# Another order of the passage between two stages, gathers asked for one block per step, and a last step in pieces

## The chip, the cores and the metric

The kernel runs on one core of a Trainium2 chip, in one launch. The metric is the device time of one execution in microseconds (us). The engines are TensorE (PE; its weight loads have a row of their own, PEld), VectorE (DVE), ScalarE (ACT), GpSimd (POOL) and SyncE (SP); each takes its instructions in program order and waits for others by semaphores. SP issues the ordinary DMAs, POOL issues the gathers and scatters by index.

## The reference

Three layers follow each other. The first is a recurrent attention over 4 x 8 heads of 768 steps and 40 dimensions, with an input gate, a forget gate and an output gate per step:

```python
m_new = np.maximum(f_gate[:, :, t] + m, i_gate[:, :, t])
C = f_stab * C + i_stab * einsum('bhd,bhe->bhde', vt, kt)
n = f_stab * n + i_stab * kt
y[:, :, t] = o * (C @ q) / max(abs(n @ q), 1)
```

Its output, 3072 rows of 320, goes through a mixture of 8 experts (hidden width 1024): a row is normed and compared with eight expert vectors, and only the best expert computes, `gate_w * (relu(x @ w1[e]) @ w2[e])`. The third layer is gated: `(sigmoid(x @ w_gate) * (x @ w_val)) @ w_out` with a hidden width of 1536. Everything is float32, the last layer's weights come as float64.

## The kernel before, in words

Products are made of float16 or bfloat16 pairs: each operand is split into a high part and what is left (low), and three products are added up. The splits are work for ScalarE (the high part, a copy) and for VectorE or GpSimd (the low part, a subtraction). The order of all instructions is written out by hand, so the order of calls in the program is the order on every engine.

**Attention.** The steps are cut into 6 chunks of 128, with 4 batches each: 24 tiles, numbered by `i`. For a tile `st_V` (GpSimd) weights V, `st_V2` splits it (copy `vh` on ScalarE, subtraction `vl` on GpSimd, for tile 22 on VectorE), `st_S` makes the scores and splits them (`ah`, `al`), `st_AV` multiplies, `st_post` divides and gates on VectorE (L574 to L567), `st_XT` turns the rows (`tp_x`), copies them (`xt`, ScalarE), squares them with a sum (L600, ScalarE) and stores them to `xs` in memory. `st_logit` makes the eight logits, `st_route` marks the best expert per row, `st_rank` counts rows per expert over a chunk and returns a list of operations (`rk`) that write the "marks" `oh_p` and `oh_b`: where in its expert's list a row stands. The last of the list is a ScalarE copy of `oh_b` (L668). `st_index` multiplies the marks into the row list (`ix_ps`), `st_first` makes the gather indices of the first expert from it.

**The passage** (from L1543 on) is the stretch in which the last four tiles (20 to 23, `t0 + 0` to `t0 + 3`) end and the first expert begins. `split_w1(0, p)` and `split_w2(0, p)` return the copies (`c10`, `c20`, ...) and the subtractions (`l10`, ...) for part `p` of the first expert's weights; a part of `w1` serves two of its eight hidden blocks. `load_w1` and `load_w2` ask for the next part over SP, once the raw buffer is read. `fill(u, n)` puts `n` matmuls on constants (L1533), whose result nobody reads. `half()` advances the first expert by half a step: its product for one hidden block (L1030 to L1034), or the activation `hh` (ScalarE, L1127), its low part `hl` (VectorE, L1128) and the second-layer products of two blocks before (L1043 to L1048).

**The experts.** They run in order of their size, with windows of 512 to 336 rows as columns; the first one in two runs of 256, the first of them over rows of all chunks but the last two. `expert_steps(n)` does run `n` in eight steps, one per hidden block `f`. In a step stand, in this order: the products, the gathers of the next run's rows (`load_x`, at `f == 0` all three or four blocks of 128 rows, L756 on GpSimd), the copies and subtractions of weight parts that come next (`w1l` L247, `w2l` L261, float64 pieces of the last layer L1212, tails `w1s` and `w2h` L216 on VectorE), and from step 3 on the scaling of the next run's gathered rows, one block a step (L990, ScalarE). From run 2 on each step takes one operation of `defer`, a list that makes the output's places: stores to `permd`, a load back, a copy to float (`pf`, L1339) and a transpose (`pn_ps`, L1314).

**The gated layer** takes 72 steps (six groups of 512 rows, twelve blocks of 128 hidden units). In a step `gated_a` and `gated_b` make gate and value products in two halves of the array at once (64 rows each), then sigmoid (L1833), product with the value (L1834), cast `hh` (L1846) and low part `hl` (L1847) follow, and `gated_l2h` multiplies by `w_out` two steps later. In the last step these four are done in two pieces of 256 columns (`col_parts`), then the output products of the last two steps follow block by block (`gated_l2`), each block is scaled (ScalarE or VectorE in turn, L1908 and L1906) and scattered to its rows by GpSimd (L1926).

Of the kernel before, what the change touches and what calls it, by code (L numbers as in the profile page):

```python
# [22 lines left out]
def kernel(  # L23
# [431 lines left out]
    def st_V2(i):  # L455
        t = vV[i]
        vh = bp.tile([P, H, DV], F16, tag="vh", name="vh")
        vl = bp.tile([P, H, DV], F16, tag="vl", name="vl")
        nc.scalar.copy(vh, t)
        (nc.vector if i == NTILE - 2 else nc.gpsimd).tensor_tensor(out=vl, in0=t, in1=vh, op=ALU.subtract)  # L460
        vV[i] = (vh, vl, t)

# [125 lines left out]

    def st_XT(i):
# [10 lines left out]
        nc.scalar.activation(out=jk, in_=xr[:, 0:DM], func=AF.Square, accum_out=ssq[:, i:i + 1])  # L600
# [683 lines left out]
    def place_ops():  # L1284
# [27 lines left out]
        def turn_back():  # L1312
# [25 lines left out]
            none,  # L1338
            lambda: v.tensor_copy(pf, pl),  # L1339
            turn_back,  # L1340
# [98 lines left out]
    def expert_steps(n):  # L1439
# [50 lines left out]
        for f in range(NF1):  # L1490
# [3 lines left out]
            if f == 0 and more:  # L1494
                load_x(n + 1)
# [53 lines left out]
    st_S(t0 + 3)  # L1549
    st_AV(t0 + 1)  # L1550
    st_logit(t0 - 1)
    st_V(t0 + 3)
    st_V2(t0 + 2)
    st_sig(t0 + 2)
    weave(c10)
    st_route(NCH - 2)
    st_post(t0 + 1)
    fill(0, 4)
    st_XT(t0)
    fill(0, 6)  # L1560
    transpose_part(0, xt[0], 0)
    st_V2(t0 + 3)
    st_sig(t0 + 3)
    weave(l10)
    load_w1(0, 2)
    fill(0, 4)
    st_AV(t0 + 2)
    weave(c20, l20)
    load_w2(0, 2)
    fill(0, 2)  # L1570
    st_logit(t0)
    rk = st_rank(NCH - 2)
    rk.pop(0)()
    transpose_part(0, xt[0], 1)
    st_post(t0 + 2)
    fill(1, 2)
    transpose_part(0, xt[0], 2)
    weave(c11[0:1], l11[0:1])
    fill(1, 2)
    st_XT(t0 + 1)  # L1580
    weave(c11[1:], l11[1:])
    load_w1(0, 3)
    fill(1, 2)
    st_AV(t0 + 3)
    st_post(t0 + 3)
    st_XT(t0 + 2)
    st_logit(t0 + 1)
    half()
    st_XT(t0 + 3)
    weave(rk)  # L1590
    half()
    st_logit(t0 + 2)
    st_logit(t0 + 3)
    st_route(NCH - 1)
    half()
    weave(c21, l21)
    load_w2(0, 3)
    rk = st_rank(NCH - 1)
    weave(rk[0:5])
    half()  # L1600
    half()
    weave(rk[5:])
    weave(*split_w1(0, 2))
    load_w1(1, 0)
    half()
    half()
    half_, low = split_w1(0, 3, nc.vector)
    weave(half_)
    st_index(NTILE - 2 * B, NTILE)
    st_first(E0 // P, GT)  # L1610
    load_x(1)
    half()
# [6 lines left out]
    half()  # L1619
    work += weight_ops()  # L1620
# [199 lines left out]
    def gated_b(t):  # L1820
        g, f = order2[t]
        fs = slice(f * P, (f + 1) * P)
        for kk in range(2):
            ins = woven(*(
                products(r, ps, w, xg[g], kk, fs, stop=(kk == 1))
                for r, ps, w in zip(halves, gv[t][::-1], gate_val[::-1])
            ))
            if kk == 0:
                turn_rows(ins[0], t)
# [9 lines left out]
    def col_parts(t):  # L1839
        return [slice(0, NM)] if t < last else [slice(u * NM // 2, (u + 1) * NM // 2) for u in range(2)]  # L1840
# [539 lines left out]
```

## Time and profile before

| | |
|---|---|
| three timed runs | 716.05 us median (714.97 to 717.76) |
| profiled execution | 710.32 us, span 708.4 us |
| busy share of the span | PE 96%, PEld 61%, DVE 60%, ACT 59%, POOL 46% |
| mean granted TensorE clock | 0.996 |
| passage and first expert run | about 113 to 151 us in the span |
| experts' runs 1 to 8 | about 150 to 343 us |
| gated layer | about 343 us to the end |

A row of a timeline gives start and length in us, engine, line of the kernel, operation, the tile written and the tiles read, the shape, and in brackets how long the engine had stood idle before it and who released it. Several like instructions in a row are merged (x6).

### The profile page before, as it was taken

To read this page: it belongs to the slowest core of one execution; us is meant where nothing else is said; L and a number is where in the kernel's file an instruction comes from. 1 tells how busy PE (TensorE), PEld (TensorE's weight loads), DVE (VectorE), ACT (ScalarE), POOL (GpSimd) and SP (SyncE) were. 2 spreads that over 40 slices of the span, in tenths; PEclk is the share of its full clock that TensorE was granted. 3 is DMA by queue.
4 is the path that set the end of the run, shared out by engine and by line. 5 is a ranking of instruction groups with operands and counts; after the bars stand their busy time and mean duration, and the time that the engine had idled before them with its cause. 6 is when DMAs were issued, how large, how long until landed. Compare 5 with 4: busy or idle time off the path is not lost. (4 is left out here: it accounts for less than half of the span.)

```text
span 708.4 us, 17936 instructions
## 1 busy us (share of the span) xinstructions
PE 681.5 (96%) x6955; PEld 434.4 (61%) x6955; DVE 424.7 (60%) x924; ACT 418.9 (59%) x1059; POOL 327.4 (46%) x392
## 2 busy tenths in 40 slices
PE   6999999899999989899999999999999999999994
PEld 5899998786445545566555555555545557755552
DVE  7978888688689998887798875252221122211111
ACT  5887876766966767678566455454555453433331
POOL 8968887544754666565010003443234324324222
PEclk9999999999999999999999999999999999999998
DMA  7756975456455557661233220010000001001001
GB/s 222 225 185 176 278 227 157 128 177 190 123 149 158 174 170 201 178 187 56 57 84 86 65 75 24 17 39 1 2 19 20 1 2 38 2 2 39 1 2 41
DMA packets 39865, 70.47 MB, mean 99 GB/s; under 512 B 4818, under 2 KB 28460, under 8 KB 39772
## 3 DMA queue, kind: packets, MB, share of 16 engines
q1 hardware_dynamic: 36764, 59.61, 28.5%
q0 software_dynamic: 3008, 9.64, 4.2%
q8 instruction: 56, 0.92, 0.5%
q14 instruction: 37, 0.30, 0.1%
HBM read 60.55 MB, written 8.68 MB: 98 GB/s over the span
## 5 line engine op out<-in xcount | busy, mean ns | idle before, releaser
L1834 DVE SCALAR_TENSOR_TENSOR sgm<-v_ps,sgm 128x512 f32<-128x512 f32 (+1 forms) x73 | 49.8, 684 | 197.1 <-ACT sgm L1833 197.0
L1847 POOL TENSOR_TENSOR hl<-sgm,hh 128x512 f16<-128x512 f32 x54 | 62.3, 1159 | 210.7 <-ACT hh L1846 210.6
L1790 PE MATMUL v_ps<-xg,wvh 64*128 64x512 f16 x288 | 108.5, 377 | 1.9 <-ACT seen L1804 1.8
L1790 PE MATMUL g_ps<-xg,wgh 64*128 64x512 f16 x288 | 108.5, 377 | 0.0
L1791 PE MATMUL g_ps<-xg,wgh 64*128 64x512 f16 x288 | 108.3, 376 | 0.0
L1791 PE MATMUL v_ps<-xg,wvh 64*128 64x512 f16 x288 | 108.3, 376 | 0.0
L1792 PE MATMUL g_ps<-xg,wgl 64*128 64x512 f16 x288 | 108.3, 376 | 0.0
L1792 PE MATMUL v_ps<-xg,wvl 64*128 64x512 f16 x288 | 108.3, 376 | 0.0
L1872 PE MATMUL o_ps<-wo,hl 64*128 64x320 f16 x560 | 86.1, 296 | 0.5 <-POOL hl L1847 0.5
L1871 PE MATMUL o_ps<-wo,hh 64*128 64x320 f16 x560 | 86.2, 296 | 0.0
L1870 PE MATMUL o_ps<-wo,hh 64*128 64x320 f16 x560 | 86.2, 296 | 0.0
L1833 ACT ACTIVATE sgm<-g_ps 128x512 f32<-128x512 f32 (+1 forms) x73 | 43.0, 591 | 72.6 <-PE g_ps L1792 72.6
L1846 ACT CAST hh<-sgm 128x512 f16<-128x512 f32 (+1 forms) x73 | 44.6, 612 | 43.5 <-DVE sgm L1834 42.7
L1804 ACT COPY seen<-zeros 1x1 f32<-1x1 f32 x142 | 26.8, 189 | 64.4 <-PE o_ps L1872 34.2
L261 POOL TENSOR_TENSOR w2l<-w2raw,w2h 128x512 bf16<-128x512 f32 x28 | 35.0, 1249 | 39.0 <-issue 19.2
L1044 PE MATMUL y_ps<-hl,w2h 128*128 128x256 f16 (+7 forms) x144 | 46.8, 325 | 3.0 <-DVE hl L1128 3.0
L1127 ACT ACTIVATE hh<-h_ps 128x256 f16<-128x256 f32 (+7 forms) x72 | 35.0, 486 | 24.2 <-PE h_ps L1034 23.8
L1032 PE MATMUL h_ps<-xh,w1l 128*128 128x256 f16 (+7 forms) x144 | 46.8, 325 | 1.0 <-POOL w1l L247 1.0
L1030 PE MATMUL h_ps<-xh,w1h 128*128 128x256 f16 (+7 forms) x144 | 46.8, 325 | 0.2 <-ACT w1h L244 0.2
L1043 PE MATMUL y_ps<-hh,w2h 128*128 128x256 f16 (+7 forms) x144 | 46.8, 325 | 0.0
L1031 PE MATMUL h_ps<-xl,w1h 128*128 128x256 f16 (+7 forms) x144 | 46.8, 325 | 0.0
L1045 PE MATMUL y_ps<-hh,w2l 128*128 128x256 f16 (+7 forms) x144 | 46.8, 325 | 0.0
(381 smaller groups left out, 1976.6 us busy)
## 6 DMA issues: line engine op xcount, KB each, us to landing
kv<-in_kvo_dram SPq DMA_DIRECT2D x24, 484.0 KB
w2raw<-in_moe_w_dram SPq DMA_DIRECT2D x32, 320.0 KB
w1raw<-in_moe_w_dram SPq DMA_DIRECT2D x32, 256.0 KB
qk<-in_qkt_dram SPq DMA_DIRECT2D x48, 160.0 KB
xs<-x SPq DMA_DIRECT2D x24, 192.0 KB
w1raw<-in_moe_w_dram SPq DMA_DIRECT2D x64, 64.0 KB
raw<-in_moe_w_out_dram SPq DMA_DIRECT2D x12, 320.0 KB
raw<-in_moe_w_gate_dram SPq DMA_DIRECT2D x8, 384.0 KB
```

Source lines behind the costliest of these rows:

```text
L1030: nc.tensor.matmul(ps, hi[:, kk, fs], h[:, kk], start=(kk == 0), stop=False)
L1031: nc.tensor.matmul(ps, hi[:, kk, fs], l[:, kk], start=False, stop=False)
L1032: nc.tensor.matmul(ps, lo[:, kk, fs], h[:, kk], start=False, stop=False)
L1043: nc.tensor.matmul(ys[d], wh, hh, start=first, stop=False)
L1790: lambda: nc.tensor.matmul(ps, at(wh), h[rows, kk], start=start, stop=False),
L1791: lambda: nc.tensor.matmul(ps, at(wh), l[rows, kk], start=False, stop=False),
L1792: lambda: nc.tensor.matmul(ps, at(wl), h[rows, kk], start=False, stop=stop),
L1834: nc.vector.scalar_tensor_tensor(out=s[:, cs], in0=pv[:, cs], scalar=2.0 ** -KH, in1=s[:, cs], op0=ALU.mult, op1=ALU.mult)
L1847: e.tensor_tensor(out=gl[:, cs], in0=s[:, cs], in1=gh[:, cs], op=ALU.subtract)
L1870: lambda: nc.tensor.matmul(o, gh[rows, ts_], wh[rows], start=begin, stop=False),
L1871: lambda: nc.tensor.matmul(o, gh[rows, ts_], wl[rows], start=False, stop=False),
L1872: lambda: nc.tensor.matmul(o, gl[rows, ts_], wh[rows], start=False, stop=end),
```

## The change

- In the passage the calls stand in another order. V of the last two tiles is weighted and copied before the scores of tile 23, and the subtraction `vl` of tile 22 is put between two operations of `st_S`. The last four tiles' output and turning come earlier, the ranks of the last-but-one chunk later. The copies of weight parts 2 and 3 of `w1` stand before the last marks of the last chunk (`rk[5:]`). Of the fillers 10 are left of 22. The squares of the last four tiles are kept in a list and made later, in twos.
- `load_x` is called for one block in each of the steps 0 to 3.
- In `place_ops` the copy `pf` stands two empty entries later, and the transpose one more entry behind it.
- In the last gated step `gated_b` makes the first half of the columns for both row pieces, then the second; `col_parts` gives 128, 128 and 256 columns; the outputs of the last group are scaled by both engines, 192 columns on ScalarE and 128 on VectorE.

```diff
@@ -452,13 +452,16 @@
         )
         vV[i] = t
 
-    def st_V2(i):
+    def st_V2(i, apart=False):
         t = vV[i]
         vh = bp.tile([P, H, DV], F16, tag="vh", name="vh")
         vl = bp.tile([P, H, DV], F16, tag="vl", name="vl")
         nc.scalar.copy(vh, t)
-        (nc.vector if i == NTILE - 2 else nc.gpsimd).tensor_tensor(out=vl, in0=t, in1=vh, op=ALU.subtract)
         vV[i] = (vh, vl, t)
+        low = lambda: (nc.vector if i == NTILE - 2 else nc.gpsimd).tensor_tensor(
+            out=vl, in0=t, in1=vh, op=ALU.subtract
+        )
+        return low if apart else low()
 
     def warm(n):
 
@@ -586,6 +589,8 @@
     def st_post(i):
         weave(post_ops(i))
 
+    squares = []
+
     def st_XT(i):
         tp = tp_ps("tp_x")
         xr = xX[i]
@@ -597,7 +602,13 @@
         if i >= NTILE - B:
             nc.scalar.copy(xr[:, DM:DX], xr[:, 2 * P:DM])
         jk = bp.tile([P, DM], F32, tag="jk", name="jk", bufs=1)
-        nc.scalar.activation(out=jk, in_=xr[:, 0:DM], func=AF.Square, accum_out=ssq[:, i:i + 1])
+        square = lambda: nc.scalar.activation(
+            out=jk, in_=xr[:, 0:DM], func=AF.Square, accum_out=ssq[:, i:i + 1]
+        )
+        if i < NTILE - B:
+            square()
+        else:
+            squares.append(square)
         nc.sync.dma_start(out=xs[i * P:(i + 1) * P, :], in_=xX.pop(i))
 
     def st_logit(i):
@@ -1336,7 +1347,10 @@
                 out=pl, in_=permd[0:NT].rearrange("(i p) o -> i (p o)", p=P)
             ),
             none,
+            none,
+            none,
             lambda: v.tensor_copy(pf, pl),
+            none,
             turn_back,
             lambda: v.tensor_copy(perm, ps[1][:, 0:NTILE]),
         ]
@@ -1491,8 +1505,8 @@
             next(run_)
             if f == NF1 - 1 and more:
                 next(run_)
-            if f == 0 and more:
-                load_x(n + 1)
+            if more and f < len(blocks(n + 1)):
+                load_x(n + 1, (f,))
             prepare(f)
             if n == 1:
                 m = min(3, len(work) - 4)
@@ -1546,69 +1560,67 @@
     st_AV(t0)
     st_post(t0)
     st_sig(t0 + 1)
-    st_S(t0 + 3)
+    st_V(t0 + 3)
+    low = st_V2(t0 + 2, True)
+    st_S(t0 + 3, None, low)
     st_AV(t0 + 1)
     st_logit(t0 - 1)
-    st_V(t0 + 3)
-    st_V2(t0 + 2)
+    st_V2(t0 + 3)
+    st_post(t0 + 1)
     st_sig(t0 + 2)
     weave(c10)
-    st_route(NCH - 2)
-    st_post(t0 + 1)
-    fill(0, 4)
+    weave(l10)
+    load_w1(0, 2)
+    fill(0, 2)
     st_XT(t0)
     fill(0, 6)
+    st_AV(t0 + 2)
+    st_sig(t0 + 3)
+    st_post(t0 + 2)
     transpose_part(0, xt[0], 0)
-    st_V2(t0 + 3)
-    st_sig(t0 + 3)
-    weave(l10)
-    load_w1(0, 2)
-    fill(0, 4)
-    st_AV(t0 + 2)
+    fill(1, 2)
+    st_AV(t0 + 3)
     weave(c20, l20)
     load_w2(0, 2)
-    fill(0, 2)
+    st_route(NCH - 2)
+    st_post(t0 + 3)
+    st_XT(t0 + 1)
     st_logit(t0)
-    rk = st_rank(NCH - 2)
-    rk.pop(0)()
     transpose_part(0, xt[0], 1)
-    st_post(t0 + 2)
-    fill(1, 2)
+    weave(c11[0:1], l11[0:1])
     transpose_part(0, xt[0], 2)
-    weave(c11[0:1], l11[0:1])
-    fill(1, 2)
-    st_XT(t0 + 1)
+    st_XT(t0 + 2)
     weave(c11[1:], l11[1:])
     load_w1(0, 3)
-    fill(1, 2)
-    st_AV(t0 + 3)
-    st_post(t0 + 3)
-    st_XT(t0 + 2)
     st_logit(t0 + 1)
-    half()
+    rk = st_rank(NCH - 2)
     st_XT(t0 + 3)
-    weave(rk)
-    half()
+    weave(rk[:-1])
     st_logit(t0 + 2)
     st_logit(t0 + 3)
+    weave(rk[-1:])
     st_route(NCH - 1)
+    half()
     half()
     weave(c21, l21)
     load_w2(0, 3)
+    half()
     rk = st_rank(NCH - 1)
     weave(rk[0:5])
     half()
-    half()
-    weave(rk[5:])
-    weave(*split_w1(0, 2))
+    c12, l12 = split_w1(0, 2)
+    weave(c12, l12)
     load_w1(1, 0)
     half()
+    acts, low = split_w1(0, 3, nc.vector)
+    weave(acts)
+    weave(rk[5:])
     half()
-    half_, low = split_w1(0, 3, nc.vector)
-    weave(half_)
+    half()
     st_index(NTILE - 2 * B, NTILE)
     st_first(E0 // P, GT)
     load_x(1)
+    weave(squares[0:2])
     half()
     half()
     weave(low)
@@ -1617,6 +1629,7 @@
     load_w2(1, 0)
     half()
     half()
+    weave(squares[2:])
     work += weight_ops()
     st_slots()
     nc.scalar.activation(out=dum, in_=zeros[:, 0:1], func=AF.Exp)
@@ -1820,13 +1833,14 @@
     def gated_b(t):
         g, f = order2[t]
         fs = slice(f * P, (f + 1) * P)
-        for kk in range(2):
-            ins = woven(*(
-                products(r, ps, w, xg[g], kk, fs, stop=(kk == 1))
-                for r, ps, w in zip(halves, gv[t][::-1], gate_val[::-1])
-            ))
-            if kk == 0:
-                turn_rows(ins[0], t)
+        for cs in ([slice(0, NM)] if t < last else [slice(u * NM // 2, (u + 1) * NM // 2) for u in range(2)]):
+            for kk in range(2):
+                ins = woven(*(
+                    products(r, ps[:, cs], w, [z[:, :, cs] for z in xg[g]], kk, fs, stop=(kk == 1 and cs.stop == NM))
+                    for r, ps, w in zip(halves, gv[t][::-1], gate_val[::-1])
+                ))
+                if kk == 0 and cs.start == 0:
+                    turn_rows(ins[0], t)
         pg, pv = gv.pop(t)
         s = mw.tile([P, NM], F32, tag="sgm", bufs=2, name="sgm")
         for cs in col_parts(t):
@@ -1837,7 +1851,7 @@
         return s
 
     def col_parts(t):
-        return [slice(0, NM)] if t < last else [slice(u * NM // 2, (u + 1) * NM // 2) for u in range(2)]
+        return [slice(0, NM)] if t < last else [slice(a, b) for a, b in ((0, P), (P, 2 * P), (2 * P, NM))]
 
     def gated_h(t, s):
         gh, gl = (mw.tile([P, NM], F16, tag=z, name=z, bufs=3) for z in ("hh", "hl"))
@@ -1901,8 +1915,12 @@
 
     back = 2.0 ** -(KX + KW - KH + KD)
 
-    def scaled_out(dst, o, j):
-        if j % 2:
+    def scaled_out(dst, o, j, both=False):
+        if both:
+            c = 3 * DM // 5
+            nc.scalar.activation(out=dst[:, 0:c], in_=o[:, 0:c], func=AF.Copy, scale=back)
+            nc.vector.tensor_scalar_mul(dst[:, c:], o[:, c:], back)
+        elif j % 2:
             nc.vector.tensor_scalar_mul(dst, o, back)
         else:
             nc.scalar.activation(out=dst, in_=o, func=AF.Copy, scale=back)
@@ -1921,7 +1939,7 @@
                     out=ot[g][:, j], in0=o, scalar=back, in1=part(g, j), op0=ALU.mult, op1=ALU.add
                 )
             else:
-                scaled_out(ot[g][:, j], o, j)
+                scaled_out(ot[g][:, j], o, j, g == NG - 1)
             i = g * G4 + j
             put = nc.gpsimd.indirect_dma_start(
                 out, bass.IndirectOffsetOnAxis(perm[:, i:i + 1], 0), ot[g][:, j], None,
```

## Rows read from the trace of the kernel before

**Rows 1.** Page: busy time of TensorE; granted clock (tenths) in 40 slices.
```profile
PE 681.5 (96%) x6955; PEld 434.4 (61%) x6955; DVE 424.7 (60%) x924; ACT 418.9 (59%) x1059; POOL 327.4 (46%) x392
...
PEclk9999999999999999999999999999999999999998
```

**Rows 2.** Waits of TensorE, whole span: total us, times, longest us.
```profile
PE y_ps L1044 <- DVE hl L1128: 3.0, 2, 1.9
PE pn_ps L1314 <- DVE y L1339: 2.0, 1, 2.0
...
PE r_ps L626 <- DVE sel L619: 0.3, 1, 0.3
...
PE h_ps L1030 <- ACT w1h L244: 0.2, 1, 0.2
```

**Rows 3.** The tile that the fillers write: count, ns, first and last start.
```profile
L1533 PE MATMUL fill_ps<-ones_bf x22: 376/379/379, 119.2 to 127.5; 128*128 128x512 bf16 x22
```

**Rows 4.** Timeline of TensorE in the passage: start, us, instruction, idle before.
```profile
120.41 1.46 PE L1533 MATMUL fill_ps<-ones_bf 128*128 128x512 bf16 x6
...
137.88 0.28 PE L704 MATMUL ix_ps<-oh_b,oh_p 128*128 128x64 bf16 x4 [0.41 <-ACT oh_b L668]
...
140.68 0.28 PE L1032 MATMUL h_ps<-xh,w1l 128*128 128x256 f16 x1 [1.00 <-POOL w1l L247]
```

**Rows 5.** Timeline of ScalarE in the passage.
```profile
128.57 0.47 ACT L600 ACTIVATE jk<-x 128x320 f32<-128x320 f32 x1
...
131.77 0.48 ACT L595 COPY xt<-tp_x 128x384 f32<-128x384 f32 x1 [0.86 <-PE tp_x L593]
...
137.46 0.37 ACT L668 ACTIVATE oh_b<-r_ps,pcol 128x128 bf16<-128x128 f32 x1 [2.39 <-DVE oh_b L667]
137.73 0.41 ACT L221 ACTIVATE w1s<-w1raw 128x256 f16<-128x256 f32 x1
...
138.61 0.62 ACT L244 CAST w1h<-w1raw 128x512 f16<-128x512 f32 x1
```

**Rows 6.** Timeline of VectorE, windows of the fifth and sixth expert.
```profile
257.35 4.92 DVE L216 SCALAR_TENSOR_TENSOR w1s<-w1raw,w1s 64x256 f16<-64x256 f32 x1
...
283.16 3.20 DVE L216 SCALAR_TENSOR_TENSOR w2h<-w2raw,w2h 128x128 f16<-128x128 f32 x1
```

**Rows 7.** Timeline of GpSimd, window of the fifth expert.
```profile
253.90 1.31 POOL L756 DMA_INDIRECT xrow<-xs,idx  x1
...
257.73 0.92 POOL L1212 TENSOR_TENSOR wvl<-fa,wvh 128x384 f16<-128x384 f32 x1
...
260.83 1.14 POOL L247 TENSOR_TENSOR w1l<-w1raw,w1h 128x512 bf16<-128x512 f32 x1
```

**Rows 8.** Timeline of all engines, the last output blocks.
```profile
696.56 0.10 PEld L1893 LDWEIGHTS <-hl 128*128 128x128 f16 x1 [0.35 <-DVE hl L1847]
...
697.62 0.99 POOL L1926 DMA_INDIRECT out_dram<-ot,perm  x1 [4.52 <-ACT ot L1908]
...
701.51 0.98 POOL L1926 DMA_INDIRECT out_dram<-ot,perm  x1 [0.31 <-issue]
```

**Rows 9.** Busy us by stretch at the end; granted clock, DMA share, GB/s last.
```profile
701.00:703.00 2.00, 0.00 (x0) 0.00 (x0) 0.00 (x0) 0.00 (x0) 1.18 (x2) 0.94 0.30 98
703.00:705.00 2.00, 0.00 (x0) 0.00 (x0) 0.00 (x0) 0.00 (x0) 0.00 (x0) 0.50 0.26 91
```

**Rows 10.** VectorE's tail subtraction of w1, all: min, median, max ns.
```profile
L216 DVE SCALAR_TENSOR_TENSOR w1s<-w1raw,w1s x29: 421/422/4921, 141.4 to 325.7; 64x256 f16<-64x256 f32 x29
```

**Rows 11.** Timeline of VectorE, then TensorE, window of the second run.
```profile
154.09 1.70 DVE L172 TENSOR_TENSOR sf_r<-sq_y,rs 128x24 f32<-128x24 f32 x1
...
166.27 0.27 PE L1044 MATMUL y_ps<-hl,w2h 128*128 128x256 f16 x1 [1.15 <-DVE hl L1128]
```

**Rows 12.** Gathers between 250 and 330 us: from start to landing.
```profile
DMA to landing us min/median/max: 3.3/3.5/4.4
```

**Rows 13.** Timeline of ScalarE, window of the seventh expert.
```profile
314.63 0.61 ACT L990 ACTIVATE xrow<-xrow,gsl 128x384 f32<-128x384 f32 x1
```

## The prediction

> **What bounds the kernel now.** I read the page's busy times first: TensorE is busy for 96% of the span [rows 1], so time is won only where TensorE stands, or where what it runs is not needed. Next the waits of TensorE, who was waited for and for how long [rows 2]: the reader is to see three that lie in what the diff touches, 3.0 us before the second expert product (two waits, the longest 1.9), 2.0 us before one small transpose, and a handful of short ones in the passage. Then the passage itself, in time order for each engine. There TensorE seems never idle, but 22 of its matmuls are fillers on constants [rows 3]; six of them take 1.46 us with the last one's 0.38 in it, so they follow each other at 0.215 us. At the end of the passage it stands for the second mark (oh_b) and for part 2 of the first-layer weights [rows 4]. ScalarE, which makes both, has two holes shortly before, 0.86 and 2.39 us [rows 5]. For the two long waits I followed VectorE and GpSimd in the windows of the fifth and sixth expert [rows 6, 7], and for the end the last output blocks [rows 8].
>
> **Passage.** The diff takes 12 of 22 fillers out (16 + 6 become 8 + 2): 12 x 0.215 = 2.6 us of TensorE [rows 3, 4]. That counts only if the chain beside it gets shorter too, so I work out both sides up to the place where TensorE starts the second half of the index products, now 137.88 [rows 4].
>
> TensorE's side: 137.88 less its own wait 0.41, less 2.6, less the 0.33 before the ranks [rows 2] = 134.5. New holes come back: the last two logit products wait for ScalarE's copies of the turned rows, which now stand behind the second weight copy; by laying the rows end to end I get about 0.35 and 0.5. It arrives near 135.4.
>
> ScalarE's side: the second mark runs at 137.46 [rows 5]. Ahead of it are moved the three copies of part 2 (from 137.73, the last at 138.61 with some 0.5 to the next, so 1.4 us) and two of part 3 (0.8 us): +2.2. Behind it go four squares, 0.47 each [rows 5]: -1.9. The two holes, 3.25 us, are now where the copies stand, for the row attention's last tiles are finished earlier (their low part of V is made before the scores' last subtraction, VectorE's ranks come later): -3.25. New holes, waiting for the last logits and the first expert product, again laid end to end: +1.0. Sum -1.9 or -2.0: the mark starts near 135.5, takes 0.37, and index goes on near 135.9. The two sides meet within half a microsecond, so neither the fillers nor the copies alone give it. Index comes 2.0 us earlier; behind it the waits of 0.25 and 1.00 for the part-2 weights [rows 2, 4] go as well, since their copies stand a whole mark earlier and GpSimd's subtractions (0.67 and 1.15 us) follow at once. That is 2.0 + 1.25 = 3.25 us. The row list of experts' second half (index, first, two gathers) moves by the same 2 to 3.5, so its small wait after it stays about as it is. Bounds: 3.85 if all fillers and waits go with only the holes of 0.85 in their place; 0 if the part-3 weights land late and hold up mark and index (no row shows when they land). I take 3.2, nearer to the upper end, as it is the one that rows carry.
>
> The fillers could be what keeps the clock up. The granted clock is full, that is 2.4 GHz, in every slice of the page up to the last [rows 1], those of the waits of 1.9 and 2.0 us with them; it falls only at the end, where TensorE does nothing after its last product at 699.0: 0.94 from 701 to 703, then 0.50, the 1.2 GHz level [rows 9]. My longest new hole is near 0.5. The Trainium skill, "TensorE: Matmul & The Clock Gate" (What's actually happening), states that an array left idle falls back to half its clock; by it fewer fillers are a risk (rival d), and the trace agrees as far as its end goes.
>
> **Rows asked one block per step.** In the fifth window GpSimd issues three gathers in a row from 253.90, 1.25 to 1.6 us each, and its four subtractions for the weights queue up: from 257.73 to 261.97 they run without a gap [rows 7]. VectorE's subtraction of the weight tail, 0.42 us in the median of 29 [rows 10], has two inputs in SBUF and takes 4.92 us, to 262.27: just until that pile is through [rows 6]. Behind it stands hl, and TensorE waits for it: 1.9 us. In the sixth window it is the same with 3.20 us, and there the copy of the places (L1339) is queued behind it, for which the transpose waits 2.0 us [rows 2]. With one gather per step the order on GpSimd is gather, two subtractions, gather, one, gather, one. VectorE gets in at the first gather: its operations beside the first two gathers of this window took their normal time. That is at 259.25 in place of 262.27 by the same rows, hl about 2.5 us earlier than now and 0.7 before TensorE asks for it. In the sixth window it gets in at 283.35, and the transpose has in addition been put two steps behind its copy, steps of 2.6 us. So 1.9 + 2.0 = 3.9 go; what is late next is hl of the fourth hidden block, which by my laying out comes 0.3 before it is wanted, so I leave 0.4 standing and take 3.5. Moved past: the later gathers now stand in front of later subtractions, each up to 1.25 us later, for weights needed two or more steps on. Bounds 1.9 and 4.0.
>
> In run 1 (second half of the first expert; the gate's factors are worked out beside it) VectorE is busy without a hole for 15 us and TensorE waits 1.15 us for it once; one small VectorE operation is stretched to 1.70 us by GpSimd's subtraction [rows 11]. The four subtractions fall on other VectorE operations after the change; I find one that loses 1.5 us less and two that lose more. I take 0, from -0.6 to +1.0.
>
> The Trainium skill, "SBUF — State Buffer" (Who interferes with whom), says that of VectorE with two SBUF inputs and GpSimd the first to start holds the pair of ports for its whole instruction. Taken alone this would let VectorE in after one subtraction. By that the pile would cost VectorE no more than one subtraction, and the spreading would win little: the 3.5 would be about 0.5 and the time 711.8. The rows show it kept out through four [rows 6, 7], so I keep 3.5.
>
> **Last gated step.** The six pairs of the value and gate products become twelve of half the columns, at 0.107 instead of 0.215 us each (by columns; 256-column products elsewhere step by 0.109): the same 1.3 us, at most 0.1 more. Sigmoid and product of the first two blocks can start before the second half is through. ScalarE does its three sigmoids before its first cast, so the first cast waits for the second half all the same, but it is then 128 columns, not 256: hh and hl of block 0 are there about 0.3 us before TensorE comes, and its waits for them, 0.35 for hl [rows 8] and about as much for hh, go. The first output's scaling, split over two engines, is 0.1 us shorter. The first scatter starts at 697.1 for 697.62. The four scatters follow each other at 1.30 us (697.62 to 701.51) [rows 8], and that row of four sets the end; it moves as a whole: 0.5 us. Bounds 0 (if the sigmoid waits for the whole bank) and 0.7.
>
> **Sum.** 3.2 + 3.5 + 0 + 0.5 = 7.2 us. The profiled execution is 710.32 us (span 708.4 and 1.9 around it), so 703.1 for one profiled like this; the median of the runs is 716.05, 5.7 above the profiled one. I apply the same difference to the median: 708.8.
>
> **Rivals.**
> (a) The pile comes back. GpSimd's three subtractions of the sixth window become ready at 282.2, 283.4 and 284.8, and would nearly touch even without gathers; if VectorE does not get in at a gather, it loses up to 1.2 us at each of them. For: VectorE was held from 257.35 on, 0.4 before the gather's row ended. Against: the normal durations beside other gathers. Price: the 3.5 shrinks to 0.5; 711.8.
> (b) The copies in front of the second mark wait for the part-3 weights, which are asked for behind GpSimd's second subtraction and compete with the row stores. Then mark, index and the second half's rows come later and the passage gives 0.5 to 1: 711.3. Against: the request is made over 1 us earlier than now, as the second subtraction ends earlier.
> (c) The other sign: the rows of a next window, asked for at the step f, are scaled by ScalarE at f + 3. A gather lands 3.3 to 4.4 us after its start [rows 12]; in the narrow windows (2.4 us a step) GpSimd comes to the third gather 4 to 5 us later than now, and the row scaling at 314.63 [rows 13] would stand before it, with every hidden block behind it. It decides from 1.2 us of wait in each of six windows, 7.2 in all; with 2 us each the time is 716.05 - 7.2 + 12 = 720.9. By my rows the third gather of the seventh window starts near 309.7 and lands at 313.0 to 314.1, 0.5 to 1.6 in front; so it costs nothing, with little to spare.
> (d) The clock falls in the passage. Half clock over the 15 us of the first expert block costs 7.5: 716.3. Against are the rows above.
> (e) The change does little: (a) and (b) together, 714.3.
>
> **Chances.** Forecast 0.60, (a) 0.13, (b) 0.12, (e) 0.09, (c) 0.04, (d) 0.02. What a measurement here can tell from no change is 0.5%, 3.6 us. Faster by more: the forecast, (a) and (b), which lie at 708.8 to 711.8, nearly whole: 0.83. Within: (e) and a rest of the others: 0.12. Slower: 0.05. The range goes from 705.8 (upper bounds: 3.85 + 4.0 + 1.0 + 0.7 = 9.6, and some scatter of the runs) to 713.0 (past (a) and (b)).
>
> **What would show it.** Passage: no filler behind about 124, index ending near 136, no wait before the fifth block's first product; a wait for oh_b over 1 us, or ScalarE standing for w1raw, means (b). Windows: no VectorE tail subtraction above 2 us, hl and the transpose gone from TensorE's waits; long ones still there mean (a). ScalarE idle in front of the row scaling, ended by a gather, means (c). A granted clock below 1.00 between 120 and 140 means (d). End: first scatter about 0.5 us nearer to the last product, no waits between the last products.

## The result, and the profile after

| | median | runs | ratio of after to before (95% interval) |
|---|---|---|---|
| before | 716.30 us | 6 (714.97 to 718.82) | |
| after | 710.18 us | 6 (709.01 to 712.18) | 0.9913 (0.9889 to 0.9937) |

The change takes 6.1 us (4.5 to 8.0 by the interval); forecast were 7.2 us and 708.8. The profiled execution after took 709.01 us (span 707.0 us), 1.2 below the median of its runs. That of before was 5.7 below the median of its first three, so the two profiles differ by 1.3 us only. Experiment 1 shows why; where sizes are compared below, its second profile of before stands beside the first.

First the waits of TensorE after (total us, times, longest), which answer to [rows 2]:

```profile
PE v_ps L1803 <- ACT seen L1817: 3.8, 8, 1.9
PE y_ps L1055 <- DVE hl L1139: 1.7, 2, 1.1
...
PE o_ps L1884 <- ACT seen L1817: 1.4, 1, 1.4
PE r_ps L637 <- ACT xt L600: 0.9, 1, 0.9
PE sp_ps L1010 <- DVE xl L216: 0.6, 1, 0.6
PE tp_x L598 <- ACT rs L622: 0.5, 1, 0.5
...
PE tp_m L1028 <- DVE perm L1355: 0.2, 1, 0.2
```

The 2.0 us before the transpose of the places are gone, and the two waits for hl that are left belong to products of run 1 (256 columns), not to the fifth window. Gone too are the waits for weight part 2. New are 0.9 and 0.5 us for copies of ScalarE in the passage. The timeline of TensorE there:

```profile
128.36 0.18 PE L637 MATMUL r_ps<-sel,tri_bf 128*128 128x32 bf16 x1 [0.88 <-ACT xt L600]
...
129.21 0.55 PE L598 MATMUL tp_x<-ident,x 128*128 128x128 f32 x3 [0.50 <-ACT rs L622]
...
132.22 0.42 PE L1041 MATMUL h_ps<-xh,w1h 128*128 128x256 f16 x1
...
137.16 0.62 PE L715 MATMUL ix_ps<-oh_b,oh_p 128*128 128x64 bf16 x8
```

For the index products no wait is listed any more, where before the second four began at 137.88 behind one of 0.41 [rows 4]. But a product of 256 columns takes 0.42 us at 132.22, where its like at 131.02 takes 0.27. The same stretch in windows of 2 us (length, busy time, granted clock, DMA share, GB/s):

```profile
130.00:132.00 2.00, 2.00 (x16) 0.88 0.77 265
132.00:134.00 2.00, 2.00 (x13) 0.50 0.80 248
134.00:136.00 2.00, 2.00 (x23) 0.76 0.00 1
```

The granted clock fell to the lower of its two levels, 1.2 GHz, for some 3 us, behind the two holes (the first slower product starts at 131.45): rival (d), to which I gave 0.02.

In the fifth window VectorE's subtraction of the weight tail takes 1.11 and 1.91 us, no longer 4.92 [rows 6]. VectorE first, with the operation that is now held longest there, then GpSimd:

```profile
255.58 1.11 DVE L216 SCALAR_TENSOR_TENSOR w1s<-w1raw,w1s 64x256 f16<-64x256 f32 x1
...
258.39 1.91 DVE L216 SCALAR_TENSOR_TENSOR w1s<-w1raw,w1s 64x256 f16<-64x256 f32 x1
...
260.61 3.05 DVE L1205 TENSOR_SCALAR fb<-raw 128x384 int32<-128x384 int32 x1
```
```profile
255.50 0.92 POOL L1223 TENSOR_TENSOR wvl<-fa,wvh 128x384 f16<-128x384 f32 x1 [2.05 <-ACT wvh L1222]
256.37 1.34 POOL L247 TENSOR_TENSOR w1l<-w1raw,w1h 128x512 bf16<-128x512 f32 x1
257.86 0.96 POOL L767 DMA_INDIRECT xrow<-xs,idx  x1
258.84 1.16 POOL L261 TENSOR_TENSOR w2l<-w2raw,w2h 128x512 bf16<-128x512 f32 x1
260.17 0.97 POOL L767 DMA_INDIRECT xrow<-xs,idx  x1 [0.16 <-issue]
261.14 1.17 POOL L247 TENSOR_TENSOR w1l<-w1raw,w1h 128x512 bf16<-128x512 f32 x1
262.26 1.17 POOL L261 TENSOR_TENSOR w2l<-w2raw,w2h 128x512 bf16<-128x512 f32 x1
```

At the end TensorE's last gate product, ScalarE's and VectorE's shares of the first output block, the first of four scatters and VectorE's share of the second block, which answer to [rows 8]:

```profile
693.00 0.27 PE L1805 MATMUL g_ps<-xg,wgl 64*128 64x256 f16 x1
695.15 0.33 ACT L1921 ACTIVATE ot<-o_ps 128x192 f32<-128x192 f32 x1 [0.16 <-PE o_ps L1907]
695.51 0.29 DVE L1922 TENSOR_SCALAR ot<-o_ps 128x128 f32<-128x128 f32 x1
696.08 0.99 POOL L1944 DMA_INDIRECT out_dram<-ot,perm  x1 [4.39 <-DVE ot L1922]
696.33 0.29 DVE L1922 TENSOR_SCALAR ot<-o_ps 128x128 f32<-128x128 f32 x1 [0.52 <-ACT ot L1921]
```

From product to scatter it is 3.08 us; before, the same distance was 3.33 (694.29 to 697.62). VectorE starts 0.03 us after ScalarE's share has ended; at the second block the row names ScalarE's share as what it waited for.

For all experiments one table of stretches, read from TensorE's timelines: from the first index product of the first half (near 112) to run 1's first row turning (`tp_m`), then from turning to turning, and the gated layer from its first gate product to the start of its last output product. Where a cell holds the clock's fall, that is said.

| kernel | passage | run 1 | 5th | 6th | 7th window | gated |
|---|---|---|---|---|---|---|
| before, first profile | 35.37 | 15.21 | 26.68 | 24.31 | 20.22 | 357.47 |
| before again (exp. 1) | 35.36 | 14.83 | 26.67 | 23.20 | 20.22 | 361.63 |
| after | 33.39, falls | 15.39 | 24.68 | 22.27 | 20.64 | 361.09 |
| passage alone (2) | 33.27, falls | 15.57 | 26.67 | 23.19 | 20.22 | 362.04 |
| windows alone (3) | 35.36, falls | 15.14 | 24.68 | 22.27 | 20.68 | 362.40 |
| last step alone (4) | 35.38 | 15.12 | 26.69 | 25.85, falls | 20.23 | 361.36 |
| holes filled (5) | 32.42 | 15.43 | 24.67 | 22.27 | 20.66 | 361.83 |
| product early (6) | 32.76, falls | 14.63 | 24.69 | 22.27 | 20.67 | 361.04 |
| gathers at once (7) | 34.90, falls | 15.11 | 26.68 | 22.26 | 20.23 | 361.11 |
| places early (8) | 33.49, falls | 15.34 | 24.68 | 22.27 | 20.22 | 361.70 |
| product and fillers (9) | 32.38 | 14.63 | 24.69 | 22.26 | 20.23 | 361.10 |
| mark first (10) | 32.08 | 14.71 | 24.68 | 22.27 | 20.23 | 361.80 |
| fewer fillers (11) | 35.39, falls | 15.13 | 26.68 | 23.19 | 20.23 | 361.67 |
| whole scaling (12) | 32.36 | 15.38 | 24.68 | 22.27 | 20.22 | 361.05 |

Run 2 takes 30.5 to 30.9 us in all eight profiles with one gather per step, and 31.4 to 31.5 in five of the six with all gathers at the first step; the first profile of before, with 30.5, is the sixth. In experiment 1 the 0.9 us more stand at two waits that a profile with one gather per step doesn't have:

```profile
173.56 0.38 PE L1043 MATMUL y_ps<-hh,w2h 128*128 128x512 f16 x1 [0.21 <-ACT hh L1127]
174.28 0.38 PE L1044 MATMUL y_ps<-hl,w2h 128*128 128x512 f16 x1 [0.35 <-DVE hl L1128]
```

Run 3 (29.1 to 30.4) varies with either order, run 4 is 26.4 and the eighth run 21.6 in all.

### The profile page after: what moved, and what is told of

Its sections match the earlier page's. It is cut to its first block, busy times and chain, and to the rows that moved or that the text cites. A ratio compares the mean times of both kernels' runs of the same rounds, so it can differ in the third digit from the quotient of the medians.

```text
span 707.0 us, 17947 instructions
## 1 busy us (share of the span) xinstructions
PE 681.2 (96%) x6955; PEld 428.1 (61%) x6955; DVE 424.8 (60%) x928; ACT 419.7 (59%) x1063; POOL 328.1 (46%) x392
## 5 line engine op out<-in xcount | busy, mean ns | idle before, releaser
L1884 PE MATMUL o_ps<-wo,hh 64*128 64x320 f16 x560 | 84.9, 296 | 1.4 <-ACT seen L1817 1.4
L1885 PE MATMUL o_ps<-wo,hh 64*128 64x320 f16 x560 | 84.9, 296 | 0.0
L247 POOL TENSOR_TENSOR w1l<-w1raw,w1h 128x512 bf16<-128x512 f32 x31 | 37.6, 1211 | 20.8 <-ACT w1h L244 19.7
L479 PE MATMUL s_ps<-qk 40*128 40x128 f32 (+1 forms) x384 | 42.1, 300 | 4.5 <-DMA qk<-in_qkt_dram 4.3
```

Source lines behind the costliest of these rows:

```text
L1884: lambda: nc.tensor.matmul(o, gh[rows, ts_], wh[rows], start=begin, stop=False),
L1885: lambda: nc.tensor.matmul(o, gh[rows, ts_], wl[rows], start=False, stop=False),
```

## Experiments

**1. The kernel before, once more.** No edit.

> The kernel before, unchanged, once more, with a profile of its own. Theory: its first profile (710.32 us) is 4.6 us shorter than its fastest timed run, and these microseconds are stray delays that most executions have and that one had not. Then the ratio is 1.000 within 0.002, the new profile reads between 714 and 717 us, and it shows the difference to the first one in a few places that the change doesn't touch. Rival: the profiled execution is shorter by its nature; then it reads 710 to 711 again, with the same waits in the same places.

714.79 us against 714.98, ratio 1.0001 (0.9987 to 1.0014); span 712.2 us. Two stops in the gated layer, where ScalarE had been away, are in this profile and not in the first. TensorE, then ScalarE:

```profile
537.15 0.39 PE L1790 MATMUL v_ps<-xg,wvh 64*128 64x512 f16 x1 [1.85 <-ACT seen L1804]
...
596.21 0.31 PE L1870 MATMUL o_ps<-wo,hh 64*128 64x320 f16 x2 [1.38 <-ACT seen L1804]
```
```profile
533.67 0.60 ACT L1833 ACTIVATE sgm<-g_ps 128x512 f32<-128x512 f32 x1 [2.66 <-remote]
```

The twelve profiles of after and of the other experiments have these two stops as well; the first profile of before alone is without, by the table 4.2 us shorter in that layer. The theory holds, and the wait in the sixth window is 0.9 here where the first profile had 2.0. What stops ScalarE is not shown by the trace ("remote" is no instruction of the kernel).

**2 to 4. Each part alone.** (2) The passage's edits; (3) `load_x` one block per step and the places later; (4) the last gated step.

> The new order of the passage alone (fillers, weight copies ahead of the last marks, squares later); gathers at the first step and the last gated step as before. Theory: the passage gives 2.0 us where its end is read (the clock at half speed for some 3 us takes 1.5 of the predicted 3.2), and run 1 keeps its waits: 1.5 to 2.5 us faster than before, ratio 0.9965 to 0.998. Rival: what the passage gives is taken back by the two waits of the fifth and sixth expert window, which follow from where GpSimd's work falls; then 0 to 1 us.

> Only the gathers asked for one block per step and the places' copy and transpose later; passage and last gated step as before. Theory: the pile on GpSimd is the cause of the two long waits; both go (VectorE's tail subtractions below 2 us, no wait of TensorE above 0.5 us in the fifth and sixth window), run 1 is unchanged or 0.5 worse: 3.0 to 4.0 us faster, ratio 0.9944 to 0.9958. Rival: the windows owe part of their gain to the passage, which moves all later work; then one of the two waits stays at over 1 us and the gain is 1.5 to 2.5.

> Only the last gated step by halves and the outputs' split scaling. Theory: the end is nearer by 0.25 us, which a comparison can't tell from nothing: ratio 0.999 to 1.000; last product to first scatter 3.1 us for 3.3. Rival: the predicted 0.5 us.

| part | ratio | by times | by the table |
|---|---|---|---|
| passage (2) | 0.9988 (0.9975 to 1.0001) | -0.9 us | -2.1 in the passage, +0.4 to +0.7 in run 1 |
| windows (3) | 0.9945 (0.9928 to 0.9962) | -3.9 us | -2.0, -0.9 (first profile: -2.0), +0.5, and -0.9 in run 2 (first profile: 0) |
| last step (4) | 0.9996 (0.9982 to 1.0010) | -0.3 us | last product to scatter 3.09 |

The sum of the three by times is 5.1 us, the whole 6.1, within the intervals. Expectations (3) and (4) were met. That of (2), 1.5 to 2.5 us, was missed: -0.9 (-1.8 to +0.1) has the size of its rival, but not for the rival's reason. In (2) the waits of the fifth window (1.89) and the sixth (0.85) stand as in experiment 1: the passage's gain is not taken back there (0.4 to 0.7 of it are missing in run 1), and by (3) the windows need nothing from the passage. In (4) the clock fell from 288 to 294 (0.79, 0.50, 0.85), behind the wait of 1.84 for the places: so this wait can cost more than its length, which neither profile of before had shown.

**5. The holes of the passage filled.**

```diff
     st_logit(t0 + 1)
+    fill(1, 4)
     rk = st_rank(NCH - 2)
+    fill(1, 2)
     st_XT(t0 + 3)
```

> The changed kernel with six more fillers (4 and 2, 0.215 us each) in the two holes that TensorE has before the ranks and before the last tile's turning in the passage (0.88 and 0.50 us); they cost 1.29 us of TensorE where it stands for 1.38. Theory: those holes bring the clock to half speed for some 3 us behind them; filled, the granted clock stays 1.00 from 130 to 136, the first expert's end comes 1.0 to 1.5 us earlier than in the changed kernel: ratio to before 0.989 to 0.990 (the changed kernel: 0.991). Rival 1: the clock falls with the fillers too, since few-column products, not the holes, lead to it; then the same time as the changed kernel or 0.2 worse. Rival 2: the clock stays up, but the second mark on ScalarE sets the index's time anyway, and nothing is gained.

Ratio 0.9886 (0.9863 to 0.9910), 708.68 us; the interval overlaps that of after, so the comparison rests on the profiles. In the passage the clock stays up:

```profile
130.00:132.00 2.00, 1.94 (x21) 1.00 0.83 202
132.00:134.00 2.00, 2.00 (x20) 1.00 0.90 313
134.00:136.00 2.00, 2.00 (x27) 1.00 0.54 181
```

and the passage is 0.97 us shorter than after (32.42 for 33.39; 1.0 to 1.5 were expected), though TensorE runs 1.29 us more of products that nobody reads. It is not the full 1.5 that the slow products cost after (16 of them, from 131.45 to 134.97 less the ranks between, take 3.26 us for 1.74 at 0.109), since TensorE now waits for the mark:

```profile
138.04 0.28 PE L715 MATMUL ix_ps<-oh_b,oh_p 128*128 128x64 bf16 x4 [0.66 <-ACT oh_b L679]
```

So both the theory and a part of rival 2 hold: with the holes filled the clock stays up, and behind that stands ScalarE's chain.

**6. The first product in the first hole.** One `half()` moved from behind `st_route(NCH - 1)` to before `rk = st_rank(NCH - 2)`.

> The changed kernel with the first expert's product for its first hidden block (eight products, 0.87 us) ahead of the ranks, so that useful work stands in the hole of 0.88 us in place of fillers. Theory: TensorE gains up to 0.65 us, and with only one hole of 0.5 left the clock stays at 1.00; together 1.0 to 2.0 us less than the changed kernel, ratio to before 0.988 to 0.990. Rival: ScalarE's row of copies before the second mark becomes what the index waits for; then TensorE waits over 0.5 us for oh_b and the gain over the changed kernel is 0.3 to 0.9.

Ratio 0.9894 (0.9870 to 0.9917). The passage is 0.63 us shorter than after, but the clock falls here too (0.50 from 132 to 134), behind holes of 0.19 and 0.30 us and at one of 0.39. The expectation's 1.0 us was not reached in the passage (it is 1.39 with run 1, whose length varies), and what it was built on didn't hold: three short holes are left, not one of 0.5.

**7 and 8. The two edits of the windows apart.** (7) all gathers at the first step again; (8) the places at their old steps.

```diff
 (7)
-            if more and f < len(blocks(n + 1)):
-                load_x(n + 1, (f,))
+            if f == 0 and more:
+                load_x(n + 1)
```

> The changed kernel with all gathers of a next window asked for at its first step, as before; passage, last gated step and the later copy of the places as changed. Theory: the pile on GpSimd is the gathers' own: VectorE's tail subtractions take over 3 us again, the fifth window's wait of 1.9 us comes back, and the sixth's is smaller than before (2.0) because the transpose waits two steps longer: 2 to 4 us slower than the changed kernel, ratio to before 0.994 to 0.997. Rival: the pile of the sixth window did not come from the gathers and the later copy of the places saves it: then about 2 us slower, 0.994.

> The changed kernel with the copy of the places and its transpose at their old steps; gathers one per step. Theory: with the pile gone the copy is in time anyway, and the later place in the list gives little: within 0.7 us of the changed kernel, ratio to before 0.991 to 0.992. Rival: at its old step the transpose still waits 1 to 2 us for the copy or for the load behind it: ratio 0.993 to 0.995.

(7) 0.9973 (0.9954 to 0.9992), (8) 0.9906 (0.9882 to 0.9931). With the gathers at once the pile is back, VectorE first, then TensorE:

```profile
257.94 4.92 DVE L216 SCALAR_TENSOR_TENSOR w1s<-w1raw,w1s 64x256 f16<-64x256 f32 x1
```
```profile
263.54 0.34 PE L1055 MATMUL y_ps<-hl,w2h 128*128 128x416 f16 x1 [1.89 <-DVE hl L1139]
```

The sixth window stays at 22.26 in (7): there the later copy is enough without the spread gathers. In (8) the spread gathers alone give both windows, and the seventh is back at 20.22. So beside the spread gathers the later places earn nothing and cost 0.4 us. All of it stands at one wait for `perm`, at the turning of the seventh run: it is listed with 0.20, but from that product on every start is 0.37 to 0.42 later than in (8). In (7), with the later places and all gathers at once, the wait is missing and the window has 20.23, so the loss takes both edits. By its ratio (7) is some 4 us slower than after, a little past the theory's 0.997. The passage of (7) is 1.5 us longer than after with nothing edited in it: its clock fell earlier (0.59 from 128 to 130) and for longer.

**9. Product early, fillers in the holes that are left, places early.**

```diff
     st_logit(t0 + 1)
+    half()
     rk = st_rank(NCH - 2)
+    fill(2, 2)
     st_XT(t0 + 3)
...
+    fill(2, 2)
     rk = st_rank(NCH - 1)
```

(with a free bank for these fillers, one `half()` less behind `st_route(NCH - 1)`, and the edit of 8).

> The changed kernel with the first hidden block's product ahead of the ranks, two fillers in each of the two holes that are left behind it (0.30 and 0.39 us), and the places' copy and transpose at their old steps. Theory: the clock stays at 1.00 through the passage; then TensorE reaches the index products about 135.1 (counted as in the changed kernel's trace) and waits 0.5 to 1.0 us for the second mark, so the passage ends 0.9 to 1.2 us earlier than in the changed kernel; the seventh window is 0.4 us shorter. Ratio to before 0.988 to 0.990. Rival: the clock falls even so; then 0.6 us in the passage and the wait for the mark under 0.3.

707.84 us, 0.9891 (0.9872 to 0.9910). The clock is 1.00 from 118 to 140, the passage 1.0 us shorter than after, the seventh window 0.4. The first four index products start at 135.17 as expected, and the wait for the mark is there:

```profile
136.38 0.28 PE L715 MATMUL ix_ps<-oh_b,oh_p 128*128 128x64 bf16 x4 [0.93 <-ACT oh_b L679]
```

**10. The mark ahead of part 3.** As 9, with `weave(acts)` of part 3 behind `weave(rk[5:])` and the next `half()`.

> As the kernel with product and fillers, and the two ScalarE copies of weight part 3 (1.0 us) behind the second mark and the activation of the third hidden block instead of ahead of the mark. Theory: with the clock up the mark is what the index waits for, and it is held by ScalarE's copies by 0.4 us only, then by VectorE: the passage ends 0.3 to 0.6 us earlier than with the copies ahead, and no wait for part 3 comes in its place (its products run 4 us later). Rival: part 3's copies or its low part come late for the seventh hidden block, and TensorE waits there 0.5 to 1 us: nothing gained or 0.5 lost.

0.9901 (0.9881 to 0.9921). The passage is 0.30 shorter than in 9, at the lower end of the theory, the wait for the mark 0.62 instead of 0.93; no wait for part 3 came. The times can't tell 9 from 10.

**11. The kernel before with fewer fillers.** Only `fill` calls are cut, 10 of 22 fillers are left.

> The kernel before with only its fillers cut, 10 of 22 left (2, 6 and 2 in the places where the changed kernel has them or nearest); order of the passage as before. Theory: the fillers stood where TensorE waits for the chain of row attention, marks and copies; without the new order the index comes at the same time within 0.4 us, TensorE has 2 to 2.6 us of holes in the fillers' place, and the clock falls behind them: within 1 us of before, ratio 0.999 to 1.0015. Rival: fillers are time that TensorE loses, and 12 x 0.215 = 2.6 us go: ratio 0.9965.

715.27 us, 1.0003 (0.9990 to 1.0016): nothing, as the theory has it. TensorE now stands where the fillers were:

```profile
126.23 0.55 PE L593 MATMUL tp_x<-ident,x 128*128 128x128 f32 x3 [0.75 <-ACT rs L611]
...
128.63 0.52 PE L593 MATMUL tp_x<-ident,x 128*128 128x128 f32 x3 [0.40 <-DVE x L567]
...
134.24 0.21 PE L626 MATMUL r_ps<-sel,tri_bf 128*128 128x32 bf16 x1 [0.90 <-DVE sel L619]
```

and the passage is 35.39 us with the clock at 0.50 from 134 to 136. In the old order even the slow clock costs nothing: it eats waits that would have come anyway (windows alone, experiment 3, shows the same, 35.36).

**12. Experiment 9 with each output block scaled by one engine.**

```diff
-                scaled_out(ot[g][:, j], o, j, g == NG - 1)
+                scaled_out(ot[g][:, j], o, j)
```

> The kernel with early product, fillers and places at their old steps, and the last outputs scaled by one engine each (320 columns, ScalarE and VectorE in turn) as in the kernel before, in place of 192 and 128 columns on both. Theory: the two halves of a split block run one after the other (0.33 and 0.29 us, VectorE released by ScalarE's write to the same tile), so the split costs 0.2 us where it was to save 0.1; undone, the first scatter comes 2.87 us after the last gate product for 3.08, and the end 0.2 us earlier; ratio to before 0.989, as a comparison of times can't tell 0.2 us. Rival: VectorE waits for something else (its three hl), and the first scatter stays at 3.1.

707.02 us, 0.9886 (0.9864 to 0.9908). Its interval overlaps that of the changed kernel, so that it is faster than that one rests on the profiles (span 705.0 for 707.0); against 9 (span 704.8) only the stretch at the end can be compared. Last gate product, first block's scaling, first scatter:

```profile
691.61 0.27 PE L1804 MATMUL g_ps<-xg,wgl 64*128 64x256 f16 x1
693.76 0.44 ACT L1925 ACTIVATE ot<-o_ps 128x320 f32<-128x320 f32 x1 [0.16 <-PE o_ps L1906]
694.47 0.99 POOL L1943 DMA_INDIRECT out_dram<-ot,perm  x1 [4.17 <-ACT ot L1925]
```

From product to scatter it is 2.86 us for 3.08: the split of the blocks had cost 0.22.

## Why the prediction was right, and where its steps were not

**In the main** the prediction was right: each of the three parts gains at the waits that it named, and the time is 1.4 us above the forecast. Of the 7.2 us 1.2 are missing in the passage and 0.25 at the end. That the other terms came out is partly luck, as shown below: two errors of the passage's sum cancel, and run 2 gives what the sixth window, in most profiles, doesn't.

**Passage: 3.2 forecast, 2.0 in the profile.** With the clock kept up (experiment 5) it is 2.95, so in its total the term is right but for the clock, which takes 1.0. The step that failed is "my longest new hole is near 0.5": I laid the new holes before the last two logit products, 0.35 and 0.5 long. They lie before the ranks (0.88) and before the last tile's turning (0.50). Both wait for a bank of the accumulator that ScalarE has still to read (its copies xt and rs): the kernel gives turning, logits and ranks two banks in turn, a use that stands in none of the operands and that I hadn't followed. Rival (d) was priced at 7.5 us for the whole first expert and given 0.02; it came with about 1.0 us in the passage. My argument against it, that the waits of 1.9 and 2.0 us had left the clock at full speed, was drawn from one execution: experiment 4 shows it falling behind just such a wait.

The mark was forecast near 135.5. Without the fall it stands at 136.1 (137.63 of experiment 5, whose first index product is 1.51 later). ScalarE's new holes, taken as 1.0 us, are 0.64, 0.67 and 0.20 us in that profile: 0.5 more. So index comes 1.3 us earlier there, not 2.0. What makes up for it is mis-sized too: the waits for part 2 went as forecast, but they were worth 1.6 us, not 1.25. The listed idle of 0.25 and 1.00 counts from the end of the product before, 0.27 after its start, where products without a wait start 0.109 apart; by the starts (138.76 to 139.28 here, 139.40 to 140.68 [rows 4]) the two waits of before hold TensorE for 0.41 and 1.17:

```profile
138.76 0.27 PE L1048 MATMUL y_ps<-hl,w2h 128*128 128x256 f16 x1
139.28 0.28 PE L1030 MATMUL h_ps<-xh,w1h 128*128 128x256 f16 x1 [0.25 <-ACT w1h L244]
139.40 0.27 PE L1031 MATMUL h_ps<-xl,w1h 128*128 128x256 f16 x1
```

From the second half of the index to run 1 it is 9.6 us in the first profile of before and 8.0 in every profile of the new order.

Experiment 11 bears out that fillers count only together with the chain beside them. Which of the calls put in another order carry the gain was not tested one by one. The hold by part-3 weights, rival (b), didn't come: ScalarE waits for no raw weights before the mark; its one such wait, 0.57 us, is at 157.04 in run 1.

**Run 1: 0 forecast.** The orders of the passage in 2, 5, 8 and after have 15.3 to 15.6 us there, before and 3, 4 and 11 have 14.8 to 15.2: some 0.3 us more, within the bounds. That the order causes it is not shown: experiments 9 and 12 have the same instructions up to there and take 14.63 and 15.38, with the whole difference at one wait for hl (0.59 in 12), and 7 has 15.11.

**Windows: 3.5 forecast.** Against the first profile they give 2.00 + 2.04 - 0.42 = 3.6, against the second 2.00 + 0.93 - 0.42 = 2.5; the times of experiment 3 say 3.9 (2.7 to 5.1). The size of the sixth window's wait is no fixed number, 0.85 to 1.96 in the five profiles with the old order there. In three of the five it is near 0.9, so the 2.0 in my sum was not the usual value. What fills the gap is run 2: 0.9 us that I had not counted, gained against every profile of the old order but the first of before. How the gathers make hh late there was not traced. The loss of 0.42 in the seventh I had not seen; it comes from the later places beside the spread gathers, which I had counted as a help. Rivals (a) and (c) didn't come: no tail subtraction above 1.91 in the fifth and sixth window (there is one of 2.48 in the seventh, above the 2 us that I had named as a sign; it was 3.65 before, and nobody waits for it), and no wait in front of the row scaling.

The reason that I gave for it was half right. I had VectorE getting in at a gather. The subtraction issued at 258.39 stood beside a gather that ran until 258.82, and still ended only at 260.30, after the next subtraction of GpSimd, where that engine has a gap of 0.16 us. The one at 255.58 got in between two subtractions that have no gap between them. The Trainium skill, "SBUF — State Buffer" (Who interferes with whom), says that the first to start holds the shared ports for its whole instruction, hence not beyond it; the row at 255.58 agrees, that at 258.39 (issued 0.45 us before the subtraction that then kept it out) and the 4.92 of experiment 7, through four subtractions, do not. What decides when VectorE gets in is not shown.

Nor is the pile gone. In the same window L1205, an operation with one input on the float64 pieces, now takes 3.05 us (0.35 in the median of 32) beside a gather and two subtractions. VectorE's 251 operations from run 2 to the eighth run together take 151.3 us after, 150.8 and 148.3 in the two profiles of before. But for L1205 nobody waits. What one gather per step does is to let the subtraction in front of `hl` through early; others are held in its place.

**End: 0.5 forecast, 0.25 measured.** The products by halves are worth 0.47 (3.33 to 2.86 in experiment 12), as worked out. The row of four scatters moves as a whole, as forecast (3.89 us from the first to the fourth in all profiles). Behind it the end varies more: from the last gate product to the end of the span it is 13.8 to 14.2 us in five profiles with the old last step and 13.6 to 14.1 in eight with the changed one. The failed step is "the first output's scaling, split over two engines, is 0.1 us shorter": VectorE waits for ScalarE's share of the same block, so 0.33 and 0.29 follow each other where one engine took 0.44. Both read one bank and write one tile; which of the two makes them wait is not shown.

**From profile to median.** I carried the 5.7 us between the profile of before and its median over to the forecast. It had a cause: 4.2 of it lie in the gated layer, most of that in the two stops of ScalarE that this one execution lacked. So the 703.1 that the sum gave for a profile came out as 709.0, and 708.8 for the median as 710.2.

## What to carry to other kernels

Fillers, or better useful products, are worth keeping where a shorter chain opens holes and nothing else is waited for behind them: here holes of 0.88 and 0.50 us cost 1.0 us by the clock, and 1.29 us of fillers in them won it back. When calls are moved, list for each the accumulator bank that it takes and who reads that bank last, and for each block that two engines share, whether one waits for the other: the waits that I missed were of these two kinds. Price a wait by the starts of the instructions around it, not by the idle time alone. And ask of an engine that is held which of its operations somebody waits for: that one has to get through early. Before a sum is made against one profile, a second profile of the same kernel shows which of its rows are fixed (the fifth window's 26.67 to 26.69 in six of six) and which move (the sixth's 23.2 to 25.9).

## What was unexpected in the hardware

- The clock does not answer to the longest hole alone. It fell in the new passage in five of five profiles without fillers in its holes (the mildest with 0.19 and 0.30 ahead of it), in none of four with them; in the old passage in two of five, once with all 22 fillers in place; and behind the wait for the places once (1.84) but not with 1.96.
- ScalarE stops twice in the gated layer, idle for 2.66 us each time in experiment 1 (the first released by "remote", the second by a gate product), which costs TensorE 1.85 to 1.93 and 1.37 to 1.40 us, in 13 of 14 profiles. The cause stays open.
